# Output weights in two loads around the last values, all heads joined in one way, and two biases loaded late in 32 pieces

## The chip, the cores and the metric

The kernel runs on one core of a Trainium2 chip. The time is device microseconds of one execution. A core has TensorE (matrix products; it reads weights by a load of its own, PEld in the profile), VectorE (DVE), ScalarE (ACT), GpSimd (POOL) and SyncE (SP), which here only issues loads and waits. Loads from HBM run on the core's 16 DMA engines. Each engine works through its own instructions in order; between engines the program synchronises with semaphores.

## The reference

One decoding step of a transformer layer for two sequences (B = 2), in float32: attention of 32 heads over a cache of 8192 keys and values of width 128, then a feed-forward layer with the squared ReLU, each with a layer norm (without gain) before it and the input added behind it.

```
x1 = layernorm(x)                                  # (2, 512)
q = x1 @ wq                                        # 32 heads of 128
p = softmax(q . k_cache * 128 ** -0.5)             # over 8192 keys
h = x + concat_heads(p @ v_cache) @ wo             # wo: (4096, 512)
z = layernorm(h) @ w1 + b1                         # w1: (512, 1792)
out = h + (max(z, 0) ** 2) @ w2 + b2               # w2: (1792, 512)
```

A pair is one head of one sequence; there are 64 pairs, numbered 0 to 63, the two sequences of a head next to each other. Each pair has 4 MB of keys and 4 MB of values; all inputs are 561 MB.

## The kernel before

Everything streams through three buffers of 64 KB per partition, `ring[0]` to `ring[2]`. First `wq` is loaded into `ring[2]`, and the small inputs (x, b1, b2, 26 values per partition) into `sm` through ScalarE's queue; then one load of 8 MB per pair, keys and values together. A loop over SyncE waits for the semaphore FREE, which VectorE raises when it has finished with a buffer, and issues the load of the pair two ahead. Pair 63 comes in pieces: its keys alone (`kld`, into `ring[0]`, L239 multiplies them), then `wo` into `ring[1]`, then its values in five pieces (`vld`, semaphores LV), then, into `ring[2]`, W1 in two pieces (3 and 1 of its 4 row blocks of 128) and W2 in four (8, 4, 1 and 1 of 14 blocks). All of these are issued by SyncE in this order and go through one queue.

Per pair, with the keys in two chunks of 4096: TensorE forms the scores (L239), spread over the 128 partitions as four groups of 32 equal rows with 1024 keys each; VectorE takes each row's negated maximum (L245, into `nm`); ScalarE forms the exponentials with their sums (L249, `ls`); VectorE multiplies them with the values and sums along the row (L254), four products per chunk, one for each 32 of the 128 value columns, eight per pair, into `ac`.

So each pair has eight partial maxima and sums. They are joined behind the loop. `stats` takes the common maximum (TensorE with `pick` at L291, VectorE at L294 and L298, ScalarE's exponential at L301) and leaves weights `wt`; `sums` and `invert` form the total of a pair and its inverse `rl` (L306, L310, L315); `folded` weights and adds the value sums and brings them into columns (L321, L324, L327). This is done twice: first for the 62 pairs of heads 0 to 30, while the last pair's values are coming in, and then, between and behind the last pair's eight products, for the two pairs of head 31.

The result of the first 62 pairs is spread 16 times (`big`, L337) and multiplied with the 31 heads of `wo` (L344), which gives the attention output as rows, spread over four groups of 32 partitions. ScalarE copies it (L348), TensorE adds the groups and turns it to columns (L351), VectorE adds it to x, in `hT` (L366). This addition stands in VectorE's queue behind the third of the last pair's eight products. Head 31 is multiplied separately (L379, L382) and added (L385). `centre` subtracts the mean (L178 to L182), `spread` forms the variance (L187 to L195), whose inverse root `rstd` is applied only behind the product with W1 (L396), as is b1 (L407 to L414). W2's products (L421) add to `h + b2`, which is put in their accumulator ahead of them (L401, L405). A copy (L426) and a store (L428) end the kernel.

The order of work on each engine is the order in which the program is written; no scheduler changes it. `take` (L61) waits for a semaphore and lowers it again.

Of the kernel before, what the change touches and what calls it, by code (L numbers as in the profile page):

```python
# [11 lines left out]
P = 128  # L12
# [15 lines left out]
W1_PIECES = [3, 1]  # L28
V_PIECES = [(0, 2), (2, 4), (4, 6), (6, 7), (7, 8)]
# [34 lines left out]
def attention_block_kernel(nc, small, kvd, wqd, kld, vld, wod, w1d, w2d, out):  # L64
# [7 lines left out]
    NS = DB * B + FB + DB  # L72
    sm = sbuf("sm", NS)
    xT = sm[:, : DB * B].rearrange("p (a b) -> p a b", b=B)
    b1T = sm[:, DB * B : DB * B + FB]
    b2T = sm[:, DB * B + FB :]
# [20 lines left out]
    o31 = sbuf("o31", B)  # L97
    xr = sbuf("xr", DB, 16, B)
    hT = sbuf("hT", DB, B)
# [15 lines left out]
    SM, LK = p.sem("small"), p.sem("k63")  # L115
    LV = [p.sem(f"v63_{k}") for k in range(len(V_PIECES))]
# [5 lines left out]
    def load(tile, src, sem):  # L122
        sp.dma_start(tile, src).then_inc(sem, 16)

# [15 lines left out]
    load(ring[2], kvd[LAST - 1], LD[2])  # L140
    p.take(sp, FREE)
    load(ring[0][:, :HALF], kld, LK)
    p.take(sp, FREE)
    load(ring[1], wod, LD[1])
    for k, (a, b) in enumerate(V_PIECES):
        load(ring[0][:, HALF + a * CS : HALF + b * CS], vld[:, a * CS : b * CS], LV[k])
    p.take(sp, FREE)
    at = 0
    for k, n in enumerate(W1_PIECES):
        load(W1[:, at : at + n], w1d[:, at : at + n], LW1[k])  # L150
        at += n
    at = 0
# [20 lines left out]
    t_c = p.tell("dve", dve.tensor_reduce(fold, ident.rearrange("p (j m) -> p m j", j=NQ), axis=AX.X, op=ALU.add))  # L173
    dve.sem_inc(BUFFER, 3)

    def centre(src, tok, bank):
        p.after("dve", tok)
        tok = p.tell("dve", dve.tensor_reduce(part, src.rearrange("p d b -> p b d"), axis=AX.X, op=ALU.add))  # L178
        p.after("pe", tok)
        tok = p.tell("pe", pe.matmul(bank[:, :B], ones_d, part, start=True, stop=True))  # L180
        p.after("dve", tok)
        tok = p.tell("dve", dve.tensor_tensor(xc, src, bank[:, None, :B].to_broadcast([P, DB, B]), op=ALU.subtract))  # L182
        p.after("dve", tok)
        return tok

    def spread(bank):
        tok = p.tell("dve", dve.tensor_tensor(sq, xc, xc, op=ALU.mult))  # L187
        p.after("dve", tok)
        tok = p.tell("dve", dve.tensor_reduce(part, sq.rearrange("p d b -> p b d"), axis=AX.X, op=ALU.add))
        p.after("pe", tok)  # L190
        tok = p.tell("pe", pe.matmul(bank[:, :B], ones_d, part, start=True, stop=True))  # L191
# [3 lines left out]
        tok = p.tell("dve", dve.reciprocal(rstd, rstd))  # L195
        return tok
# [3 lines left out]
    tok = centre(xT, t_c, pm[0])  # L200
    tok = spread(pm[1])
# [83 lines left out]
    t_m = p.tell("dve", dve.tensor_copy(hT, xT))  # L285

    def stats(lo, nb):
        n2 = slice(lo * NC, (lo + nb) * NC)
        p.after("pe", t_m)
        for j in range(NQ):  # L290
            ins = pe.matmul(pm[0][:, j * nb * NC : (j + 1) * nb * NC], pick[:, j, :], nm[:, n2], start=True, stop=True)  # L291
        tok = p.tell("pe", ins)
        p.after("dve", tok)
        tok = p.tell("dve", dve.tensor_reduce(gm[:, lo : lo + nb], pm[0][:, : NQ * nb * NC].rearrange(  # L294
            "p (j i c) -> p i j c", j=NQ, c=NC), axis=AX.XY, op=ALU.min))
        p.after("dve", tok)
        w3 = wt[:, n2].rearrange("p (i c) -> p i c", c=NC)
        tok = p.tell("dve", dve.tensor_tensor(w3, gm[:, lo : lo + nb, None].to_broadcast([P, nb, NC]),  # L298
                                              nm[:, n2].rearrange("p (i c) -> p i c", c=NC), op=ALU.subtract))
        p.after("act", tok)  # L300
        return p.tell("act", act.activation(wt[:, n2], wt[:, n2], AF.Exp))  # L301

    def sums(lo, nb, tok):
        n2 = slice(lo * NC, (lo + nb) * NC)
        p.after("dve", tok)
        tok = p.tell("dve", dve.tensor_tensor(lw[:, n2], ls[:, n2], wt[:, n2], op=ALU.mult))  # L306
        p.after("pe", tok)
        l3 = lw[:, n2].rearrange("p (i c) -> p i c", c=NC)
        for c in range(NC):
            ins = pe.matmul(pm[1][:, :nb], pick_all, l3[:, :, c], start=(c == 0), stop=(c == NC - 1))  # L310
        return p.tell("pe", ins)

    def invert(lo, nb, tok):
        p.after("dve", tok)
        return p.tell("dve", dve.reciprocal(rl[:, lo : lo + nb], pm[1][:, :nb]))  # L315

    def folded(lo, nb):
        aw4 = aw[:, lo * NC * NH : (lo + nb) * NC * NH].rearrange("p (i c e) -> p i c e", c=NC, e=NH)
        ac4 = ac[:, lo * NC * NH : (lo + nb) * NC * NH].rearrange("p (i c e) -> p i c e", c=NC, e=NH)
        w4 = wt[:, lo * NC : (lo + nb) * NC].rearrange("p (i c) -> p i c", c=NC)[:, :, :, None].to_broadcast([P, nb, NC, NH])  # L320
        tok = p.tell("dve", dve.tensor_tensor(aw4, ac4, w4, op=ALU.mult))  # L321
        p.after("dve", tok)
        as3 = acs[:, lo * NH : (lo + nb) * NH].rearrange("p (i e) -> p i e", e=NH)
        tok = p.tell("dve", dve.tensor_tensor(as3, aw4[:, :, 0, :], aw4[:, :, 1, :], op=ALU.add))  # L324
        p.after("pe", tok)
        for e in range(NH):
            ins = pe.matmul(pm[0][32 * e : 32 * e + 32, :nb], fold, as3[:, :, e], start=True, stop=True)  # L327
        return p.tell("pe", ins)

    tok = stats(0, NG)  # L330
    tok = sums(0, NG, tok)
    tok = invert(0, NG, tok)
    p.after("dve", tok)
    tok = folded(0, NG)
    p.after("dve", tok)
    o4 = big[:, : HG * 32].rearrange("p (h r b) -> p h r b", r=16, b=B)
    tok = p.tell("dve", dve.tensor_tensor(  # L337
        o4, pm[0][:, :NG].rearrange("p (h b) -> p h b", b=B)[:, :, None, :].to_broadcast([P, HG, 16, B]),
        rl[:, :NG].rearrange("p (h b) -> p h b", b=B)[:, :, None, :].to_broadcast([P, HG, 16, B]), op=ALU.mult))
    p.after("pe", tok)  # L340
    p.take(pe, LD[1], 16)
    for h in range(HG):
        j = h % NQ
        ins = pe.matmul(pm[1][32 * j : 32 * j + 32, :], big[:, h * 32 : h * 32 + 32], WO[:, h, :],  # L344
                        start=(h < NQ), stop=(h + NQ >= HG))
    tok = p.tell("pe", ins)
    p.after("act", tok)
    tok = p.tell("act", act.activation(acc, pm[1], AF.Copy))  # L348
    p.after("pe", tok)
    for d in range(DB):  # L350
        ins = pe.matmul(pm[0][:, d * B : (d + 1) * B], acc[:, d * P : (d + 1) * P], fold[:, :B], start=True, stop=True)  # L351
    t_h = p.tell("pe", ins)


    order = [(c, e) for c in range(NC) for e in range(NH)]
    t_w = t_l = None
    piece = {a: k for k, (a, b) in enumerate(V_PIECES)}
    for n, (c, e) in enumerate(order):
# [15 lines left out]
    t_v = p.tell("dve", ins)  # L374
    t_z = p.tell("act", act.activation(s[2][:, :P], zero.to_broadcast([P, P]), AF.Copy))
    p.after("dve", t_v)
    tok = folded(NG, B)
    p.after("dve", tok)
    tok = p.tell("dve", dve.tensor_tensor(o31, pm[0][:, :B], rl[:, NG:BH], op=ALU.mult))  # L379
    p.after("pe", tok)  # L380
    for d in range(DB):
        ins = pe.matmul(pm[1][:, d * B : (d + 1) * B], WO[:, H - 1, d * P : (d + 1) * P], o31, start=True, stop=True)  # L382
    tok = p.tell("pe", ins)
    p.after("dve", tok)
    tok = p.tell("dve", dve.tensor_tensor(hT, hT, pm[1][:, : DB * B].rearrange("p (d b) -> p d b", b=B), op=ALU.add))  # L385
    tok = centre(hT, tok, pm[0])
    tok = p.tell("dve", dve.tensor_copy(xr, xc[:, :, None, :].to_broadcast([P, DB, 16, B])))
    p.after("pe", tok)
    y = s[0][:, :FQ]
    o = s[2][:, :P]  # L390
    at_d = 0
    for k, n in enumerate(W1_PIECES):
# [6 lines left out]
        if k == 0:  # L399
            t_r = spread(pm[1])  # L400
            t_b = p.tell("dve", dve.tensor_tensor(hb, hT, b2T[:, :, None].to_broadcast([P, DB, B]), op=ALU.add))  # L401
# [6 lines left out]
    p.after("dve", tok)  # L408
# [54 lines left out]
```

## Time and profile before

| What | Time |
|---|---|
| Median of three runs | 1309.69 us (1308.71 to 1312.11) |
| Profiled execution | 1312.31 us |
| its span, first to last instruction | 1309.7 us |
| TensorE busy | 410.1 us (31%) |
| VectorE busy | 759.0 us (58%) |
| ScalarE busy | 160.2 us (12%) |
| Mean DMA rate over the span | 428 GB/s |

The shares are means over the span; what an engine waits for has to be read stage by stage. In a row of a timeline the first two numbers are the start and the duration in us, then come engine, line, operation, what is written and read, and in brackets the idle time before it with what ended it. `DVEq`, `PEq` and `SPq` are the sequencers of the engines; a wait at L61 is mostly for a load. Rows for stretches of time give busy time of PE, PEld, DVE, ACT and POOL with numbers of instructions, then the granted TensorE clock as a share of the full one, the mean busy share of the 16 DMA engines, and GB/s. A product in float32 stands as two matmul records.

### The profile page before, as it was taken

The page shows a single profiled execution, that of the slowest core. Times are in us where ns is not written, and L with a number is a line of the kernel's source. Part 1 is how long each engine was busy: PE and PEld are TensorE (multiplying, and loading weights), DVE is VectorE, ACT ScalarE, POOL GpSimd, SP SyncE. Part 2 cuts the span into 40 slices and gives each one's busy share as a digit, 9 for nine tenths or more (in the row PEclk, how much of TensorE's full clock was granted, in tenths as well). Part 3 has the DMA queues.
Part 4 walks back from the last instruction along what each step waited for, and adds up shares of the span by engine and source line. Part 5 has one row for each costly group of instructions (what it writes and reads, how often), then busy time and mean ns, then how long its engine had stood idle before and what let it go on. Part 6 is the DMA issues. An engine that isn't in the chain of part 4 may idle for free. (4 is left out here: it accounts for less than half of the span.)

```text
span 1309.7 us, 8250 instructions
## 1 busy us (share of the span) xinstructions
PE 410.1 (31%) x2390; PEld 112.6 (9%) x2390; DVE 759.0 (58%) x1227; ACT 160.2 (12%) x267; POOL 0.7 (0%) x6
## 2 busy tenths in 40 slices
PE   2323223323323323332331332332232233133156
PEld 0100000000000000000000000000000000000013
DVE  1465575565566466557556556655645755664663
ACT  0011011011111111101101111110110110111110
POOL 0000000000000000000000000000000000000000
PEclk9766566656666566656666666766666675666667
DMA  9999999999999999999999999999999999999996
GB/s 417 417 447 422 442 438 426 444 422 444 420 444 420 446 418 446 420 444 436 428 444 420 446 420 444 420 444 420 446 418 446 428 436 442 422 444 422 430 423 271
DMA packets 11381, 561.14 MB, mean 428 GB/s; under 512 B 1392, under 2 KB 1520, under 8 KB 2160
## 3 DMA queue, kind: packets, MB, share of 16 engines
q1 hardware_dynamic: 11232, 561.06, 99.1%
q8 instruction: 3, 0.05, 0.0%
q10 hardware_dynamic: 144, 0.01, 0.0%
q14 instruction: 2, 0.02, 0.0%
HBM read 561.00 MB, written 0.07 MB: 428 GB/s over the span
## 5 line engine op out<-in xcount | busy, mean ns | idle before, releaser
L239 PE MATMUL s<-ring,qc 128*32 128x512 f32 x2048 | 369.8, 888 | 852.0 <-PEq L61 852.0
L254 DVE SCALAR_TENSOR_TENSOR ring<-ring,s 128x1024 f32<-128x1024 f32 x512 | 589.5, 1217 | 3.7 <-DVEq L61 3.6
L245 DVE TENSOR_REDUCE nm<-s 128x1024 f32 (+1 forms) x128 | 156.7, 1225 | 488.4 <-DVEq L61 488.4
L249 ACT ACTIVATE s<-s,nm 128x1024 f32<-128x1024 f32 x128 | 139.3, 1088 | 1081.8 <-ACTq L61 1081.8
L239 PEld LDWEIGHTS s<-ring,qc 128*32 128x32 f32 x2048 | 93.0, 155 | 1128.5 <-issue 1128.5
L254 DVE DVE_READ_ACCUMULATOR ring<-ring,s (+1 forms) x512 | 42.5, 83 | 0.0
L249 ACT ACTIVATION_READ_ACCUMULATOR s<-s,nm (+1 forms) x128 | 24.7, 193 | 0.0
L178 DVE TENSOR_REDUCE part<-sm 128x2 f32<-128x8 f32 x1 | 0.2, 161 | 19.3 <-DVEq L61 19.3
L344 PE MATMUL pm<-ring,big 128*32 128x512 f32 x62 | 10.0, 798 | 2.4 <-PEq L61 2.4
L216 PE MATMUL s<-ring,xr 128*32 128x512 f32 x64 | 9.7, 773 | 2.3 <-issue 2.3
L180 PE MATMUL pm<-part,ones_d 128*128 128x2 f32 x4 | 1.2, 363 | 23.6 <-DVE part L178 23.6
L221 DVE STREAM_TRANSPOSE big<-s 128x512 f32<-128x512 f32 x2 | 1.4, 718 | 9.1 <-PE s L216 9.1
L396 PE MATMUL s<-ring,xr 128*32 128x448 f32 x32 | 5.9, 886 | 0.6 <-issue 0.6
L270 DVE COPY qc<-qs 128x96 f32 x21 | 5.1, 243 | 0.0
L195 DVE RECIPROCAL rstd<-rstd 128x2 f32<-128x2 f32 x2 | 0.3, 166 | 7.7 <-ACT rstd L193 7.7
L291 PE MATMUL pm<-nm,pick 128*128 128x124 f32 (+1 forms) x16 | 3.3, 357 | 4.5 <-DVE hT L285 4.3
L193 ACT ACT_TABLE_LOAD x1 | 1.3, 1283 | 25.1 <-PE pm L191 25.1
L421 PE MATMUL s<-ring,a 128*2 128x128 f32 x112 | 3.2, 272 | 1.3 <-issue 1.3
L310 PE MATMUL pm<-lw,pick_all 128*128 128x62 f32 (+1 forms) x8 | 2.1, 395 | 4.6 <-DVE lw L306 4.6
L344 PEld LDWEIGHTS pm<-ring,big 128*32 128x32 f32 x62 | 2.6, 139 | 9.1 <-issue 9.1
L366 DVE TENSOR_TENSOR hT<-hT,pm 128x8 f32<-128x8 f32 x1 | 0.2, 164 | 5.6 <-PE pm L351 5.6
L291 PEld LDWEIGHTS pm<-nm,pick 128*128 128x128 f32 x16 | 2.9, 271 | 5.7 <-DVE hT L285 5.4
(63 smaller groups left out, 37.1 us busy)
## 6 DMA issues: line engine op xcount, KB each, us to landing
ring<-in_kld SPq DMA_DIRECT2D x1, 4096.0 KB, 31.1
ring<-in_vld SPq DMA_DIRECT2D x3, 1024.0 KB, 36.3
ring<-in_w1d SPq DMA_DIRECT2D x1, 2688.0 KB, 28.7
ring<-in_w2d SPq DMA_DIRECT2D x1, 2048.0 KB, 35.1
ring<-in_vld SPq DMA_DIRECT2D x2, 512.0 KB, 39.7
ring<-in_w2d SPq DMA_DIRECT2D x1, 1024.0 KB, 34.1
ring<-in_kvd SPq DMA_DIRECT2D x63, 40.9
ring<-in_w1d SPq DMA_DIRECT2D x1, 896.0 KB, 30.5
```

The costliest lines, as they stand in the source:

```text
L216: ins = pe.matmul(s[0][32 * j : 32 * j + 32, n * 512 : n * 512 + 512], xs[:, d, :], ring[2][:, c0 : c0 + 512], start=(d == 0), stop=(d == ...
L221: tok = p.tell("dve", dve.transpose(big[:, n * 512 : n * 512 + 512], s[0][:, n * 512 : n * 512 + 512]))
L239: ins = pe.matmul(s[k][32 * j : 32 * j + 32, n * 512 : (n + 1) * 512], qc[:, u, :], slot[:, c0 : c0 + 512], start=True, stop=True)
L245: dve.tensor_reduce(at(nm, pair, NC, c, 1), s[k], axis=AX.X, op=ALU.max, negate=True).then_inc(MAXED, 1)
L249: act.activation(s[k], s[k], AF.Exp, bias=at(nm, pair, NC, c, 1), scale=1.0, accum_out=at(ls, pair, NC, c, 1)).then_inc(EXPED, 1)
L254: return dve.scalar_tensor_tensor(v, v, 1.0, s[k], op0=ALU.mult, op1=ALU.mult, accum_out=at(ac, pair, NC * NH, c * NH + e, 1))
L270: dve.tensor_copy(qc, qs[:, bass.ds(i + 3, 3)][:, :, None].to_broadcast([P, 3, 32])).then_inc(QUERY, 1)
L291: ins = pe.matmul(pm[0][:, j * nb * NC : (j + 1) * nb * NC], pick[:, j, :], nm[:, n2], start=True, stop=True)
L310: ins = pe.matmul(pm[1][:, :nb], pick_all, l3[:, :, c], start=(c == 0), stop=(c == NC - 1))
L344: ins = pe.matmul(pm[1][32 * j : 32 * j + 32, :], big[:, h * 32 : h * 32 + 32], WO[:, h, :], start=(h < NQ), stop=(h + NQ >= HG))
L396: ins = pe.matmul(y[32 * j : 32 * j + 32, :], xs[:, d, :], W1[:, d, j * FQ : (j + 1) * FQ], start=(d == 0), stop=(d == DB - 1))
L421: ins = pe.matmul(o[32 * j : 32 * j + B, :], a2[:, m, :], W2[:, m, j * P : (j + 1) * P], start=False, stop=(m == FB - 1))
```

## The change

Loads. `sm` holds x alone. b2 is loaded by SyncE behind pair 62's keys and values, before it waits for the buffer of the last keys; b1 behind W1 and before W2. Each comes in 16 loads of 15, 14, 13 and so on to 1, and then 8 partitions, of 16 bytes (b2) or 56 bytes (b1) per partition, each with a semaphore of its own. `wo` comes as 24 heads ahead of the last values and 8 heads behind them; the last values come in three pieces (3, 3 and 2 products' worth) instead of five, W1 in 2 + 2 row blocks instead of 3 + 1.

Joining. The maxima, weights and totals of all 64 pairs are formed at once, behind the last pair's maxima; VectorE first waits for b2's 16 semaphores and adds b2 to x (`xb`). `folded` still runs twice, for 62 pairs and for the last two, but both end in `big`. The projection with `wo` runs for heads 0 to 23, then, behind the last pair's `folded`, for 24 to 30 and 31, all in the same accumulator. VectorE's last eight products follow each other with only the waits for values between.

Layer norm. ScalarE's copy of the projected rows also sums them; one more product of these sums with a constant matrix `foldm` gives the mean, so that `hc` (the centred x plus the attention output) minus the mean is written straight into `xr`. The variance comes from `xr`. `h + b2` is one addition of `xb`. Before the transposition behind W1, VectorE waits for b1's 16 semaphores. The load of ScalarE's square root table and the zeroing of W2's accumulator move ahead of the products.

The core of the diff:

```diff
-W1_PIECES = [3, 1]
-V_PIECES = [(0, 2), (2, 4), (4, 6), (6, 7), (7, 8)]
+W1_PIECES = [2, 2]
+V_PIECES = [(0, 3), (3, 6), (6, 8)]
+HA = 24
+ROW_PIECES = [15, 14, 13, 12, 11, 10, 9, 8, 7, 6, 5, 4, 3, 2, 1, 8]
...
+    def load_rows(tile, src, sems):
+        at = 0
+        for n, sem in zip(ROW_PIECES, sems):
+            load(tile[at : at + n], src[at : at + n], sem)
+            at += n
...
     load(ring[2], kvd[LAST - 1], LD[2])
+    load_rows(b2T, bias2, LB2)
     p.take(sp, FREE)
     load(ring[0][:, :HALF], kld, LK)
     p.take(sp, FREE)
-    load(ring[1], wod, LD[1])
+    load(WO[:, :HA], wod[:, :HA], LD[1])
     for k, (a, b) in enumerate(V_PIECES):
         load(ring[0][:, HALF + a * CS : HALF + b * CS], vld[:, a * CS : b * CS], LV[k])
+    load(WO[:, HA:], wod[:, HA:], LO)
     p.take(sp, FREE)
...
+    load_rows(b1T, bias1, LB1)
...
-    t_m = p.tell("dve", dve.tensor_copy(hT, xT))
+    for sem in LB2:
+        p.take(dve, sem, 16)
+    t_m = p.tell("dve", dve.tensor_tensor(xb, xT, b2T[:, :, None].to_broadcast([P, DB, B]), op=ALU.add))
...
+    def projected(lo, hi):
+        for h in range(lo, hi):
+            j = h % NQ
+            ins = pe.matmul(pm[1][32 * j : 32 * j + 32, :], big[:, h * 32 : h * 32 + 32], WO[:, h, :],
+                            start=(h < NQ), stop=(h + NQ >= H))
+        return ins
...
+    tok = folded(0, NG)
     p.after("pe", tok)
     p.take(pe, LD[1], 16)
+    projected(0, HA)
...
     for n, (c, e) in enumerate(order):
...
         ins = product(c, LAST, c, e, ring[0])
-        if n == 2:
-            p.after("dve", t_h)
-            t_h = p.tell("dve", dve.tensor_tensor(hT, hT, pm[0][:, : DB * B].rearrange("p (d b) -> p d b", b=B), op=ALU.add))
-            t_m = t_h
-            t_w = stats(NG, B)
-        if n == 4:
-            t_l = sums(NG, B, t_w)
-            act.activation(warm, eps_t, AF.Sqrt)
-        if n == 5:
-            t_l = invert(NG, B, t_l)
...
+    t_o = folded(NG, B)
+    p.take(pe, LO, 16)
+    projected(HA, HG)
+    p.after("pe", t_o)
+    tok = p.tell("pe", projected(HG, H))
+    p.after("act", tok)
+    tok = p.tell("act", act.activation(acc, pm[1], AF.Copy, accum_out=rows))
...
+    mean = s[2][:, 512 : 512 + B]
+    t_n = p.tell("pe", pe.matmul(mean, rows.to_broadcast([P, P]), foldm, start=True, stop=True))
+    tok = p.tell("dve", dve.tensor_tensor(hc, xc, h3, op=ALU.add))
+    tok = p.tell("dve", dve.tensor_tensor(xr, hc[:, :, None, :].to_broadcast([P, DB, 16, B]),
+                                          mean[:, None, None, :].to_broadcast([P, DB, 16, B]), op=ALU.subtract))
...
+    for sem in LB1:
+        p.take(dve, sem, 16)
     p.after("dve", t_y)
     tok = p.tell("dve", dve.transpose(yT, y))
```

More of the change, by code (lines that the diff above doesn't have):

```diff
@@ L61, in take, with attention_block_kernel @@
         engine.wait_ge(sem, n).then_inc(sem, -n)
-def attention_block_kernel(nc, small, kvd, wqd, kld, vld, wod, w1d, w2d, out):
+def attention_block_kernel(nc, small, bias1, bias2, kvd, wqd, kld, vld, wod, w1d, w2d, out):
     p = Program(nc)
@@ L71, in attention_block_kernel @@
     ring = [sbuf(f"ring{s}", ROW) for s in range(3)]
[L72 to L76, printed above, removed]
+    sm = sbuf("sm", DB * B)
+    xT = sm.rearrange("p (a b) -> p a b", b=B)
+    b1T = sbuf("b1T", FB)
+    b2T = sbuf("b2T", DB)
     ones_d = sbuf("ones_d", P)
@@ L96, in attention_block_kernel @@
     acc = sbuf("acc", D)
-    o31 = sbuf("o31", B)
+    rows = sbuf("rows", 1)
+    foldm = sbuf("foldm", B)
+    xb = sbuf("xb", DB, B)
+    hc = sbuf("hc", DB, B)
     xr = sbuf("xr", DB, 16, B)
-    hT = sbuf("hT", DB, B)
     hb = sbuf("hb", DB, B)
@@ L115, in attention_block_kernel @@
     SM, LK = p.sem("small"), p.sem("k63")
+    LO = p.sem("wo_b")
+    LB1 = [p.sem(f"bias1_{k}") for k in range(len(ROW_PIECES))]
+    LB2 = [p.sem(f"bias2_{k}") for k in range(len(ROW_PIECES))]
     LV = [p.sem(f"v63_{k}") for k in range(len(V_PIECES))]
@@ L173, in attention_block_kernel, with squares, root @@
     t_c = p.tell("dve", dve.tensor_reduce(fold, ident.rearrange("p (j m) -> p m j", j=NQ), axis=AX.X, op=ALU.add))
+    p.after("dve", t_c)
+    t_c = p.tell("dve", dve.tensor_scalar(foldm, fold[:, :B], 1.0 / D, None, op0=ALU.mult))
     dve.sem_inc(BUFFER, 3)
-    def centre(src, tok, bank):
+    def squares(src, tok):
         p.after("dve", tok)
-        tok = p.tell("dve", dve.tensor_reduce(part, src.rearrange("p d b -> p b d"), axis=AX.X, op=ALU.add))
-        p.after("pe", tok)
-        tok = p.tell("pe", pe.matmul(bank[:, :B], ones_d, part, start=True, stop=True))
+        tok = p.tell("dve", dve.tensor_tensor(sq, src, src, op=ALU.mult))
         p.after("dve", tok)
[L182 to L189, printed above, removed]
+        return p.tell("dve", dve.tensor_reduce(part, sq.rearrange("p d b -> p b d"), axis=AX.X, op=ALU.add))
+    def root(bank, tok):
         p.after("pe", tok)
@@ L194, in spread @@
         p.after("dve", tok)
-        tok = p.tell("dve", dve.reciprocal(rstd, rstd))
-        return tok
+        return p.tell("dve", dve.reciprocal(rstd, rstd))
     p.after("act", t_c)
     p.take(dve, SM, 16)
-    tok = centre(xT, t_c, pm[0])
-    tok = spread(pm[1])
+    p.after("dve", t_c)
+    tok = p.tell("dve", dve.tensor_reduce(part, xT.rearrange("p d b -> p b d"), axis=AX.X, op=ALU.add))
+    p.after("pe", tok)
+    tok = p.tell("pe", pe.matmul(pm[0][:, :B], ones_d, part, start=True, stop=True))
+    p.after("dve", tok)
+    t_x = p.tell("dve", dve.tensor_tensor(xc, xT, pm[0][:, None, :B].to_broadcast([P, DB, B]), op=ALU.subtract))
+    tok = root(pm[1], squares(xc, t_x))
     p.after("dve", tok)
@@ L284, in attention_block_kernel @@
         maxes(c, LAST, c)
-    t_m = p.tell("dve", dve.tensor_copy(hT, xT))
[L287 to L315, printed above, removed]
+    for sem in LB2:
+        p.take(dve, sem, 16)
@@ new lines, in attention_block_kernel, with by_pair @@
+    t_m = p.tell("dve", dve.tensor_tensor(xb, xT, b2T[:, :, None].to_broadcast([P, DB, B]), op=ALU.add))
+    def by_pair(t):
+        return t.rearrange("p (i c) -> p i c", c=NC)
+    p.after("pe", t_m)
+    for j in range(NQ):
+        ins = pe.matmul(pm[0][:, j * BH * NC : (j + 1) * BH * NC], pick[:, j, :], nm, start=True, stop=True)
+    tok = p.tell("pe", ins)
+    p.after("dve", tok)
+    tok = p.tell("dve", dve.tensor_reduce(gm, pm[0].rearrange("p (j i c) -> p i j c", j=NQ, c=NC), axis=AX.XY, op=ALU.min))
@@ new lines, in attention_block_kernel @@
+    p.after("dve", tok)
+    tok = p.tell("dve", dve.tensor_tensor(by_pair(wt), gm[:, :, None].to_broadcast([P, BH, NC]), by_pair(nm), op=ALU.subtract))
+    p.after("act", tok)
+    tok = p.tell("act", act.activation(wt, wt, AF.Exp))
+    act.activation(warm, eps_t, AF.Sqrt)
+    t_z = p.tell("act", act.activation(s[2][:, :P], zero.to_broadcast([P, P]), AF.Copy))
+    p.after("dve", tok)
+    tok = p.tell("dve", dve.tensor_tensor(lw, ls, wt, op=ALU.mult))
+    p.after("pe", tok)
+    for c in range(NC):
+        ins = pe.matmul(pm[1][:, :BH], pick_all, by_pair(lw)[:, :, c], start=(c == 0), stop=(c == NC - 1))
@@ L317, in folded @@
+    tok = p.tell("pe", ins)
+    p.after("dve", tok)
+    t_l = p.tell("dve", dve.reciprocal(rl, pm[1][:, :BH]))
     def folded(lo, nb):
@@ L319, in folded @@
         ac4 = ac[:, lo * NC * NH : (lo + nb) * NC * NH].rearrange("p (i c e) -> p i c e", c=NC, e=NH)
-        w4 = wt[:, lo * NC : (lo + nb) * NC].rearrange("p (i c) -> p i c", c=NC)[:, :, :, None].to_broadcast([P, nb, NC, NH])
+        w4 = by_pair(wt[:, lo * NC : (lo + nb) * NC])[:, :, :, None].to_broadcast([P, nb, NC, NH])
         tok = p.tell("dve", dve.tensor_tensor(aw4, ac4, w4, op=ALU.mult))
@@ L327, in folded @@
             ins = pe.matmul(pm[0][32 * e : 32 * e + 32, :nb], fold, as3[:, :, e], start=True, stop=True)
[L328 to L333, printed above, removed]
-    tok = folded(0, NG)
[L335 to L339, printed above, removed]
+        tok = p.tell("pe", ins)
+        p.after("dve", tok, t_l)
+        n = nb // B
+        return p.tell("dve", dve.tensor_tensor(
+            big[:, lo * 16 : (lo + nb) * 16].rearrange("p (h r b) -> p h r b", r=16, b=B),
+            pm[0][:, :nb].rearrange("p (h b) -> p h b", b=B)[:, :, None, :].to_broadcast([P, n, 16, B]),
+            rl[:, lo : lo + nb].rearrange("p (h b) -> p h b", b=B)[:, :, None, :].to_broadcast([P, n, 16, B]), op=ALU.mult))
+    def projected(lo, hi):
[4 more added lines that the diff above has]
+        return ins
+    tok = folded(0, NG)
     p.after("pe", tok)
     p.take(pe, LD[1], 16)
[L342 to L352, printed above, removed]
+    projected(0, HA)
     order = [(c, e) for c in range(NC) for e in range(NH)]
-    t_w = t_l = None
     piece = {a: k for k, (a, b) in enumerate(V_PIECES)}
@@ L363, in attention_block_kernel @@
         ins = product(c, LAST, c, e, ring[0])
-        if n == 2:
-            p.after("dve", t_h)
-            t_h = p.tell("dve", dve.tensor_tensor(hT, hT, pm[0][:, : DB * B].rearrange("p (d b) -> p d b", b=B), op=ALU.add))
-            t_m = t_h
-            t_w = stats(NG, B)
-        if n == 4:
-            t_l = sums(NG, B, t_w)
-            act.activation(warm, eps_t, AF.Sqrt)
-        if n == 5:
-            t_l = invert(NG, B, t_l)
[L374 to L377, printed above, removed]
-    p.after("dve", tok)
-    tok = p.tell("dve", dve.tensor_tensor(o31, pm[0][:, :B], rl[:, NG:BH], op=ALU.mult))
+    tok = p.tell("dve", ins)
+    p.after("dve", tok)
+    t_o = folded(NG, B)
[3 more added lines that the diff above has]
+    tok = p.tell("pe", projected(HG, H))
+    p.after("act", tok)
+    tok = p.tell("act", act.activation(acc, pm[1], AF.Copy, accum_out=rows))
     p.after("pe", tok)
+    h2 = pm[0][:, : DB * B]
     for d in range(DB):
[L382 to L387, printed above, removed]
+        ins = pe.matmul(h2[:, d * B : (d + 1) * B], acc[:, d * P : (d + 1) * P], fold[:, :B], start=True, stop=True)
+    t_h = p.tell("pe", ins)
+    mean = s[2][:, 512 : 512 + B]
+    t_n = p.tell("pe", pe.matmul(mean, rows.to_broadcast([P, P]), foldm, start=True, stop=True))
+    h3 = h2.rearrange("p (d b) -> p d b", b=B)
+    p.after("dve", t_h)
+    tok = p.tell("dve", dve.tensor_tensor(hc, xc, h3, op=ALU.add))
+    p.after("dve", t_n, tok)
+    tok = p.tell("dve", dve.tensor_tensor(xr, hc[:, :, None, :].to_broadcast([P, DB, 16, B]),
+                                          mean[:, None, None, :].to_broadcast([P, DB, 16, B]), op=ALU.subtract))
     p.after("pe", tok)
+    t_q = squares(xr[:, :, 0, :], tok)
+    t_b = p.tell("dve", dve.tensor_tensor(hb, xb, h3, op=ALU.add))
     y = s[0][:, :FQ]
@@ L399, in attention_block_kernel @@
         if k == 0:
-            t_r = spread(pm[1])
-            t_b = p.tell("dve", dve.tensor_tensor(hb, hT, b2T[:, :, None].to_broadcast([P, DB, B]), op=ALU.add))
+            t_r = root(pm[1], t_q)
     t_y = p.tell("pe", ins)
@@ L405, in attention_block_kernel @@
         pe.matmul(o[32 * j : 32 * j + B, :], hb[:, j, :], ident, start=True, stop=False)
+    for sem in LB1:
+        p.take(dve, sem, 16)
     p.after("dve", t_y)
     tok = p.tell("dve", dve.transpose(yT, y))
-    p.after("dve", tok)
+    p.after("dve", tok, t_r)
     y3 = yT.rearrange("p (m r) -> p m r", r=32)
@@ L445 @@
     arrays = {
-        "small": np.concatenate([x, a(B_b1).reshape(NQ, FB, 32).transpose(0, 2, 1).reshape(P, FB), a(B_b2).reshape(DB, P).T], axis=1),
+        "small": x,
+        "bias1": a(B_b1).reshape(NQ, FB, 32).transpose(0, 2, 1).reshape(P, FB),
+        "bias2": a(B_b2).reshape(DB, P).T,
         "kvd": np.concatenate([k[:LAST], v[:LAST]], axis=2),
@@ L450 @@
         "vld": v[LAST],
-        "wod": a(A_wo).reshape(H, DH, D).transpose(1, 0, 2).reshape(P, H * D),
+        "wod": a(A_wo).reshape(H, DH, D).transpose(1, 0, 2),
         "w1d": a(B_w1).reshape(DB, P, F).transpose(1, 0, 2),
```

## The prediction

> **What bounds the kernel now.** I read the page's totals first, then the stage table, then the chain that ended last, then the loads. No engine is near full, the transfers are:
>
> ```profile
> span 1309.7 us, 8250 instructions
> PE 410.1 (31%) x2390; PEld 112.6 (9%) x2390; DVE 759.0 (58%) x1227; ACT 160.2 (12%) x267; POOL 0.7 (0%) x6
> ```
>
> The stage table (engines' busy time, then TensorE clock, DMA share, GB/s) says where that stops being true:
>
> ```profile
> 60.00:1230.00 1170.00, 353.17 (x1952) 89.05 (x1952) 700.48 (x1102) 145.19 (x241) 0.00 (x0) 0.63 1.00 434
> ...
> 1260.00:1290.00 30.00, 16.88 (x102) 8.57 (x102) 14.53 (x30) 5.10 (x10) 0.00 (x0) 0.64 0.99 417
> ...
> 1297.00:1298.00 1.00, 1.00 (x8) 0.22 (x4) 0.00 (x0) 0.00 (x0) 0.00 (x0) 0.50 0.78 279
> ...
> 1298.80:1299.20 0.40, 0.40 (x8) 0.22 (x4) 0.00 (x0) 0.00 (x0) 0.00 (x0) 0.50 0.19 72
> ...
> 1299.60:1300.00 0.40, 0.40 (x8) 0.17 (x4) 0.00 (x0) 0.00 (x0) 0.00 (x0) 0.50 0.00 0
> ```
>
> All input is in by about 1299.9 us; until 1298 nearly all 16 DMA engines move, and in the last 1.6 us a fifth of them (three). The remaining 9.8 us are computation that came too late. The change leaves the 561 MB as they are, so the stream is a floor, and the gain can only be in those 9.8 us. The chain through them, from the landing of the output weights on (start, duration, what):
>
> ```profile
> 1272.52 10.02 PE pm L344 x62
> ...
> 1282.55 0.61 ACT acc L348
> ...
> 1283.20 1.07 PE pm L351 x8
> ...
> 1287.19 1.22 DVE ring L254 x3
> ...
> 1290.87 1.23 DVE ring L254 x3
> ...
> 1293.12 1.88 PE pm L382 x8
> ...
> 1295.43 0.59 PE pm L180 x2
> ...
> 1296.59 4.71 PE s L396 x24
> ...
> 1301.29 0.52 PE pm L191 x2
> 1301.81 1.16 PE s L396 x8
> ...
> 1304.46 3.28 PE s L421 x112
> ...
> 1307.77 0.29 DVE res L426
> ```
>
> After the projection of 31 heads (L344) VectorE still has five of the last pair's eight products (L254) to do: they stand in its queue behind the sum hT at L366, which waits for that projection. Everything behind them is late by that.
>
> **The loads.** SyncE's issues (start, duration), and KB and time to landing:
>
> ```profile
> 1202.14 0.34 SPq L123 DMA_DIRECT2D ring<-in_kvd  x1
> 1221.91 0.34 SPq L123 DMA_DIRECT2D ring<-in_kld  x1
> 1240.16 0.33 SPq L123 DMA_DIRECT2D ring<-in_wod  x1
> 1240.54 2.32 SPq L123 DMA_DIRECT2D ring<-in_vld  x5
> 1260.18 0.80 SPq L123 DMA_DIRECT2D ring<-in_w1d  x2
> 1261.02 14.11 SPq L123 DMA_DIRECT2D ring<-in_w2d  x4
> 1308.08 0.35 SPq L428 DMA_DIRECT2D out<-res  x1
> ...
> ring<-in_kld SPq DMA_DIRECT2D x1, 4096.0 KB, 31.1
> ...
> ring<-in_w1d SPq DMA_DIRECT2D x1, 2688.0 KB, 28.7
> ring<-in_w2d SPq DMA_DIRECT2D x1, 2048.0 KB, 35.1
> ...
> out<-res SPq DMA_DIRECT2D x1, 64.0 KB, 1.5
> ...
> ring<-in_wod SPq DMA_DIRECT2D x1, 32.2
> ```
>
> Last keys land at 1221.9 + 31.1 = 1253.0, output weights (8192 KB) at 1240.2 + 32.2 = 1272.4, so 8192 KB take 19.4 us, or 2.42 us per 1024 KB. W1's first 2688 KB land at 1260.2 + 28.7 = 1288.9, so the values ahead of them end 6.4 us earlier, at 1282.5, and W1's last 896 KB 2.1 us later, at 1291.0; W2's first 2048 KB at 1261.0 + 35.1 = 1296.1 and its last at about 1299.9.
>
> **The change, part by part.**
>
> *Output weights in 24 + 8 heads with the values between.* Same bytes, other order: 24 heads are 6144 KB, in at 1253.0 + 14.5 = 1267.5. The values come 3, 3 and 2 x 512 KB: 1271.2, 1274.8, 1277.2. The other eight heads follow at about 1282.5, where the values ended before.
>
> *One soft-max weighting for all 64 pairs.* 124 columns become 128. Before, it is this (start, duration):
>
> ```profile
> 1260.44 2.35 DVE L245 TENSOR_REDUCE nm<-s 128x1 f32<-128x1024 f32 x2 [0.40 <-DVEq L61]
> ...
> 1270.17 1.19 DVE L337 TENSOR_TENSOR big<-pm,rl 128x992 f32<-128x992 f32 x1 [0.56 <-PE pm L327]
> ...
> L61 DVEq EVENT_SEMAPHORE  x262: 21/21/21, 22.9 to 1289.8; - x131
> ```
>
> It ends at 1271.4, and with 3% more columns still by 1271.5. The copy of eight columns behind the maxima becomes a sum of eight columns behind 16 more waits. A wait is 21 ns by the last row; with dispatch I take 50 ns, 0.8 us, which passes while the second maximum (1.2 us of the 2.35) still runs. If that cover were missing, 0.8 us come on a step that has slack: the products behind it are weighted 0.5 us before they are needed (below). The second weighting of the last pair alone goes away, and with it the two halts inside the products.
>
> *The products.* VectorE starts them at 1271.5, 1.2 us each (1290.87 to 1292.1): 1281.0, as all three pieces are in time. The weighting of the pair then takes what it takes before between 1292.1 and 1293.12, 1.0 us: 1282.0. So the last values are no longer the limit; the second load of output weights at 1282.5 is.
>
> *Projection.* The 48 records of 24 heads run from 1271.5 and are done by 1280.5 even at the pace of before (62 in 10.02 us). What is left at 1282.5 is 8 heads, 16 records. Their price depends on the granted clock:
>
> ```profile
> 1272.50:1278.44 5.94, 5.92 (x28) 1.56 (x32) 3.33 (x5) 0.00 (x0) 0.00 (x0) 0.50 1.01 416
> 1278.44:1282.60 4.16, 4.06 (x38) 1.07 (x30) 0.26 (x2) 0.05 (x1) 0.00 (x0) 1.00 1.04 429
> ...
> 1296.50:1301.20 4.70, 4.61 (x24) 1.12 (x24) 0.22 (x2) 0.00 (x0) 0.00 (x0) 0.50 0.33 122
> ...
> 1304.40:1307.80 3.40, 3.24 (x112) 2.90 (x112) 0.04 (x1) 0.00 (x0) 0.00 (x0) 1.00 0.00 0
> ```
>
> Half clock 0.21 us a record, full clock 0.11. TensorE will have idled about 2 us, as it had before 1285, so I take half: 3.4 us, to 1286.0. Evacuation 0.61 plus the read-out of the row sums now collected with it, 0.2:
>
> ```profile
> L249 ACT ACTIVATION_READ_ACCUMULATOR s<-s,nm (+1 forms) x128 | 24.7, 193 | 0.0
> ```
>
> That is 1286.9. Back to columns, 8 small products: 1.07 us at full clock, 1.88 for eight such (L382) at half; I take 1.9: 1288.8. The mean is one more product, 0.6 like L180; the sum hc goes beside it. Then xr, an estimated 0.3 us from L180's neighbours at 1296.02 to 1296.59: 1289.7. L382 and the separate mean of hT (L178 to L182) go.
>
> *W1 in 2 + 2.* Its first half (1792 KB) lands at 1286.8, before 1289.7: no wait. 16 records at half clock (24 in 4.71) 3.1: 1292.8. The variance product 0.5, second half (in since 1291.0) 3.1: 1296.4. From there the chain of before holds, 1302.97 to 1304.46, 1.5 us: W2's products start at 1297.9. W2's first part is in, the last comes at 1299.9. 3.28 us: 1301.2. As before, 2.0 us follow (1304.46 + 3.28 to 1309.7). End 1303.1, which is 6.6 us less. With the full clock everywhere, the last piece of W2 would be the limit: 1299.9 + 0.3 + 2.0 = 1302.2, 7.5 us less. If W2's 112 records too ran at half clock, 3.3 us more: 1306.4, 3.3 less.
>
> *The biases, 32 small loads.* Issue: 0.33 to 0.46 us each by the rows above (five in 2.32), so 5 to 7.5 us for 16. The first group is issued after 1202.5 and SyncE has nothing to do until 1221.9; the second before W2's, whose data is needed from 1291 on. The issue itself is hidden up to 1.2 us per load. What the pieces cost in the stream no row shows. One engine may get a row and a completion from each of 16 pieces, for each bias: 32 times both. Lower bound, from the old load of small inputs:
>
> ```profile
> q10 hardware_dynamic: 144, 0.01, 0.0%
> ```
>
> under 0.05% of 16 x 1309.7 us is under 10.5 us for 144 packets, under 73 ns each; pipelined row and completion cost 0 to 0.15 us together, 0 to 4.7 us on that engine. Upper bound: if each piece waits for its own landing, the lone output store's 1.5 - 0.35 = 1.15 us, 37 us. I take the lower row, since these are reads under running traffic as that one was, and in its range a low value, 0.05 us, as 73 ns is what the rounding leaves and no measurement: 1.6 us, about what most engines have spare against the slowest three (1298 to 1299.6 above). Net: 0. A gain below zero is possible only as far as those three lose their share of the old small load, under 0.3 us.
>
> The Trainium skill (DMA: Bandwidth & Descriptors, section Rules for kernel authors) speaks against it: many small transfers should be coalesced into one large one. Its section Anatomy of one DMA gives about 2.0 us of fixed cost per DMA, fitted for loads issued by GpSimd, where these come from SyncE; 32 of them in series would be an estimated 64 us. This trace has 12 loads landing between 1260 and 1300 with the DMA share at 0.99 to 1290, so such a cost overlaps here, at least for loads of 256 KB and more; for loads of a few rows no run here shows it.
>
> **Against the median.** The profiled execution took 1312.31 us (span 1309.7 and 2.6 around it), 0.2% over the median 1309.69. I take the 6.6 us off the median: 1303.1.
>
> **Rivals.**
> 1. *The small loads go one landing at a time* on one DMA engine, and every later load waits for that engine. With price c per piece, the end moves by 32c - 1.6. The gain is eaten at c = 0.25; slower by 0.3% (3.9 us) from c = 0.38 us; at 1.15 it would be 1338. For it: nothing here shows small loads back to back. Against it: W2's last three loads, 1536 KB, end 3.8 us after its first, and the rate alone makes it 3.6. The Trainium skill (same title, section Queues, rings and completion order) says the semaphore write lands only after every earlier write of that engine, which is how this could come about; no run here shows a stall by it.
> 2. *SyncE's queue fills.* W2's four issues took 14.11 us with eight loads outstanding. If it is the number of loads that blocks, the first 16 pieces hold up the keys' issue till 1241.6 and then the last eight pieces' issue, 8 x 0.4 = 3 us of stream, is lost, and as much again ahead of W2: 6 us, time 1309. Against it: those four issues were over by 1275.1, when only the weights (1272.4) and at most one piece of the values (2.4 us later) had landed, so it is not one landing per issue.
> 3. *TensorE stays at half clock throughout:* 3.3 us gained, 1306.4.
>
> **How the numbers follow.** What a measurement of this kernel can tell is about 0.3%, 3.9 us: faster is under 1305.8, slower over 1313.6. Forecast (1301.5 to 1305.5) 0.58; rival 3 in between, half of it still faster, 0.14; rival 2 and rival 1 with c near 0.25 (1306 to 1313) 0.13; rival 1 beyond 0.38, 0.15. Faster 0.58 + 0.07 + 0.03 = 0.68, same 0.17, slower 0.15. The range goes from just under the full-clock floor (1302.2, and 0.7 for the spread of the runs) to 1310, with 0.18 left out above. The forecast's own range is that of its case.
>
> **What would show it.** DMA share falling to zero at 1299 to 1301, and under 4 us after it to the end (9.8 now); all eight last products in one run, starting near 1271.5; the last eight heads starting at the second load's landing near 1282.5; W2's products starting before 1298.5; the waits for biases under 0.3 us. Wrong if the keys land later than 1254, or a hole in the DMA share stands near 1242 or 1291, or W2 lands after 1302.

## The result and the profile after

Over 20 runs of each, the changed kernel takes 1307.93 us and the kernel before 1310.47 us, medians; the ratio is 0.9981 (95% interval 0.9975 to 0.9988). It is faster, by 2.5 us and not by 6.6. The profiled execution took 1307.91 us with a span of 1306.2.

The computation went as forecast, and further. The rows of the changed kernel's timeline (start, duration, engine, line, what):

```profile
1263.15 0.16 DVE L302 TENSOR_TENSOR xb<-sm,b2T 128x8 f32<-128x8 f32 x1
...
1281.73 0.17 DVE L332 TENSOR_TENSOR aw<-ac,wt 128x16 f32<-128x16 f32 x1
...
1283.24 3.47 PE L350 MATMUL pm<-ring,big 128*32 128x512 f32 x16 [0.84 <-PEq L63]
1286.77 0.60 ACT L374 ACTIVATE acc<-pm 128x512 f32<-128x512 f32 x1 [18.26 <-PE pm L350]
...
1287.51 1.05 PE L378 MATMUL pm<-fold,acc 128*128 128x2 f32 x8 [0.81 <-ACT acc L374]
...
1289.27 2.73 PE L398 MATMUL s<-ring,xr 128*32 128x448 f32 x16 [0.48 <-issue]
...
1292.44 2.07 PE L398 MATMUL s<-ring,xr 128*32 128x448 f32 x16
...
1295.77 0.19 DVE L417 SCALAR_TENSOR_TENSOR a<-a 128x28 f32<-128x28 f32 x1
```

All is ready for W2 at 1295.96 us, where before it was 1304.4. But TensorE then stands still. The whole chain that ended last is these lines:

```profile
1299.33 0.04 issue
1299.37 4.95 PE s L424 x112
1304.32 0.02 issue
1304.34 0.29 DVE res L429
```

The chain begins at 1299.3, with the landing of W2's first part. SyncE's issues and the times to landing of the changed kernel:

```profile
1202.94 5.70 SPq L129 DMA_DIRECT2D b2T<-in_bias  x16
1220.66 0.36 SPq L129 DMA_DIRECT2D ring<-in_kld  x1
...
1261.46 10.61 SPq L129 DMA_DIRECT2D b1T<-in_bias  x16
1272.11 11.61 SPq L129 DMA_DIRECT2D ring<-in_w2d  x4
```

```profile
ring<-in_kld SPq DMA_DIRECT2D x1, 4096.0 KB, 33.2
...
ring<-in_w2d SPq DMA_DIRECT2D x1, 2048.0 KB, 27.1
```

```profile
L129 SPq DMA_DIRECT2D ring<-in_w2d x4: 351/3486/4161, 1272.1 to 1280.0; - x4
DMA to landing us min/median/max: 22.9/26.8/29.2
```

The keys land at 1220.66 + 33.2 = 1253.8 instead of 1253.0, W2's first part at 1272.1 + 27.1 = 1299.2 instead of 1296.1, its last at 1280.0 + 22.9 = 1302.9 instead of 1299.9. The bytes are the same, so something holds the stream up by 3 us. Stretches of time (the last three columns are TensorE clock, DMA share, GB/s) show how:

```profile
1297.00:1298.00 1.00, 0.00 (x0) 0.00 (x0) 0.00 (x0) 0.00 (x0) 0.00 (x0) 1.00 0.77 311
1298.80:1299.20 0.40, 0.00 (x0) 0.00 (x0) 0.00 (x0) 0.00 (x0) 0.00 (x0) 1.00 0.47 189
1299.60:1300.00 0.40, 0.40 (x24) 0.39 (x16) 0.00 (x0) 0.00 (x0) 0.00 (x0) 1.00 0.51 205
1302.00:1302.40 0.40, 0.40 (x16) 0.31 (x12) 0.00 (x0) 0.00 (x0) 0.00 (x0) 0.50 0.07 26
```

Before, the share fell from 0.78 (1297 to 1298) to 0.19 (from 1298.8) and to zero at 1299.6: thirteen engines ended nearly together. Now half of the engines still work at 1299.6 and one at 1302.2. The engines end one after another, and a load is complete when the last of them is: W2's first part lands on the first engine at 1294.0 and on the last at 1299.2, and TensorE starts at 1299.4. Landings on single engines, here and below, are the times at which each engine signals a load's semaphore in the trace.

### The profile page after: what moved, and what is told of

Its sections match the earlier page's. It is cut to its first block, busy times and chain, and to the rows that moved or that the text cites. A ratio compares the mean times of both kernels' runs of the same rounds, so it can differ in the third digit from the quotient of the medians.

```text
span 1306.2 us, 8270 instructions
## 1 busy us (share of the span) xinstructions
PE 411.9 (32%) x2372; PEld 110.4 (8%) x2372; DVE 757.6 (58%) x1221; ACT 160.2 (12%) x267; POOL 0.7 (0%) x6
## 5 line engine op out<-in xcount | busy, mean ns | idle before, releaser
L253 PE MATMUL s<-ring,qc 128*32 128x512 f32 x2048 | 375.7, 900 | 848.7 <-PEq L63 848.7
L424 PEld LDWEIGHTS s<-ring,a 128*2 128x2 f32 x112 | 3.9, 109 | 5.7 <-issue 4.9
## 6 DMA issues: line engine op xcount, KB each, us to landing
ring<-in_kld SPq DMA_DIRECT2D x1, 4096.0 KB, 33.2
ring<-in_w2d SPq DMA_DIRECT2D x1, 2048.0 KB, 27.1
```

The lines of the kernel that those rows point to most:

```text
L253: ins = pe.matmul(s[k][32 * j : 32 * j + 32, n * 512 : (n + 1) * 512], qc[:, u, :], slot[:, c0 : c0 + 512], start=True, stop=True)
L424: ins = pe.matmul(o[32 * j : 32 * j + B, :], a2[:, m, :], W2[:, m, j * P : (j + 1) * P], start=False, stop=(m == FB - 1))
```

## The experiments

Three theories. Theory 1 is the prediction's first rival in a mild form: the small loads pass one after another on a DMA engine, at some 0.18 us each. That is the spacing at which one engine completes its pieces of b1 in the trace of the changed kernel (the last engine twelve of them from 1291.92 to 1293.94). Theory 2: the 16 issues ahead of W2 make SyncE late (W2's issues begin at 1272.1 instead of 1261.0). Theory 3: the new order and cutting of the large loads costs stream time. Ratios are to the kernel before, on the same chip.

**Biases early, the rest of the change kept.**

```diff
+    sm = sbuf("sm", DB * B + FB + DB)      # x, b1 and b2 in one load at the start, as before
-    load_rows(b2T, bias2, LB2)
-    load_rows(b1T, bias1, LB1)
-    for sem in LB2: p.take(dve, sem, 16)   # and the same for LB1
```

> The changed kernel with both biases back in the one small load at the start; everything else of the change stays. Theory 1 (the 16 small pieces pass one after another on a DMA engine, 0.18 us each, and delay all later loads on it): W2's last landing back from 1302.9 to about 1299.9 us, span about 1303, ratio to before 0.995. Theory 2 (SyncE issues W2 too late, 1272 to 1284 instead of 1261 to 1275): the same, since the 16 issues are gone. Theory 3 (the new order and cutting of the large loads costs stream time): W2's landing stays at 1302 to 1303, span about 1306, ratio 0.998.

Measured: 1303.6 us, ratio 0.9951 (0.9938 to 0.9965), span 1302.1. Its interval lies wholly below that of the changed kernel: the rest of the change gains 6.4 us, and the late biases cost 3.9 (0.0030 in the ratio; 4.1 between the spans). W2 in this kernel:

```profile
L128 SPq DMA_DIRECT2D ring<-in_w2d x4: 432/1807/4378, 1261.2 to 1266.6; - x4
DMA to landing us min/median/max: 33.0/35.6/36.7
```

```profile
1298.42 0.04 issue
1298.46 1.68 PE s L411 x48
1300.14 0.02 issue
1300.16 0.29 DVE res L416
```

The last piece lands at 1266.6 + 33.0 = 1299.6, as before the change, and the last product ends 0.6 us later. Theory 3 falls. This version beats both kernels.

**Each bias in one load, at the late places.**

```diff
-ROW_PIECES = [15, 14, 13, 12, 11, 10, 9, 8, 7, 6, 5, 4, 3, 2, 1, 8]
+ROW_PIECES = [128]
```

> The changed kernel with each bias in one load of 128 rows, at the places where the 16 loads stood. Theory 1, if the price hangs on the number of loads (completions) per engine: one completion in the place of 16, at most 0.4 us left, span about 1303.3. Theory 1, if the price hangs on the rows: 8 rows per engine and bias, 8 x 0.18 = 1.4 us twice, on all engines alike, span about 1305.5. Theory 2: two issues in the place of 32, span about 1303.

Measured: 1303.65 us, ratio 0.9953 (0.9940 to 0.9967), span 1302.2. Late places cost nothing, and 128 rows in one load cost nothing that can be seen: on the first engine to finish, b1 lands 0.21 us behind W1's second half, and W2's first part is 0.09 us later behind W1 than with the biases early. So the price hangs on the number of loads, not on the rows.

**One bias late at a time.** The other bias goes back to the small load at the start.

```diff
-    load_rows(b2T, bias2, LB2)      # first run: b1 alone stays late
-    load_rows(b1T, bias1, LB1)      # second run: b2 alone stays late
```

> The changed kernel with b2 back in the small load at the start and b1 still in 16 late pieces ahead of W2. Theory 1: half of the loss stays, W2's last landing about 1301.3, span about 1304.7, ratio 0.9965. Theory 2: the issues ahead of W2 are all there, so the whole loss stays: landing 1302.9, span 1306, ratio 0.998.

> The changed kernel with b1 back in the small load at the start and b2 still in 16 late pieces ahead of the last keys. Theory 1: half of the loss stays, keys about 1 us later than 1253.0, W2's last landing about 1301, span about 1304.5, ratio 0.9963. Theory 2: W2 is issued early as before, nothing is lost: landing 1299.9, span about 1303, ratio 0.995.

Measured: 1305.08 us, ratio 0.9965 (0.9951 to 0.9978) with b1 alone late, and 1305.93 us, 0.9965 (0.9952 to 0.9979) with b2 alone. W2's last piece lands at 1301.65 and 1301.31, against 1299.56 with both early and 1302.94 with both late. Each group costs about half, 1.8 us by the ratios; the intervals overlap that of the first experiment, but the landings lie apart. In the second run W2's issues begin at 1260.35, and it loses as much as the first: theory 2 is not what happens here. In the changed kernel too, the last of W2's issues is over at 1283.7, before the first engine has W1's first half (1284.8).

A second cause shows in the landings of single engines. Behind W1's first half, where no small load stands between two others, each engine keeps its distance to the first one within 0.1 us. But in both runs the slowest one falls back once: from 2.59 to 3.56 us between W1 and W2's first part with b2 alone late, from 3.08 to 4.01 between W2's first and second part with b1 alone late. Just then, from 1293.07 and from 1297.14, the trace has a packet of 8 KB on the queue q14, which brings instructions of the program. The pages count these packets over the span, of the changed kernel and of the one with the biases early:

```profile
q14 instruction: 2, 0.02, 0.0%
```

```profile
q14 instruction: 1, 0.01, 0.0%
```

The runs without a late packet (biases early, each bias in one load, and the last experiment) have no such step. The kernel before has one, at 1294.03, but there an engine with room fell back, from 0.91 to 1.89, and the last landing hardly moved. In the changed kernel the packet comes at 1293.61, and the slowest engine is then 1.0 us behind the next. So of the 3.4 us by which W2's last landing moved, an estimated 1.0 goes with this packet and 2.4 with the small loads themselves. That the packet takes the time is inferred from when it comes; no run moved it alone.

**The kernel before with late biases alone.**

```diff
     load(ring[2], kvd[LAST - 1], LD[2])
+    load_rows(b2T, bias2, LB2)             # b1 behind W1 likewise, the waits as in the changed kernel
```

> The kernel before with the bias part of the change alone: b2 and b1 each late in 16 pieces, nothing else. Theory 1: keys and output weights land about 1 us later, the chain behind the output weights starts that much later, W2 (3 us later) is still in time there: span about 1310.8, ratio 1.0008. Theory 2: W2 is issued later but needed only at 1304, nothing ahead of it moves: ratio 1.000.

Measured: 1313.38 us, ratio 1.0023 (1.0014 to 1.0032), span 1312.0. Worse than either theory expected, and for another reason. The output weights come 0.9 us later, as theory 1 had it, but the projection behind them ran 0.8 us faster at a better clock, and the product with W1 ends at 1302.6, no later than before (1303.0). The loss comes behind it, from a cost that I had put at nothing (start, duration):

```profile
1302.15 0.15 DVE L413 TENSOR_TENSOR hb<-hT,b2T 128x8 f32<-128x8 f32 x1
1303.87 0.65 DVE L421 STREAM_TRANSPOSE yT<-s 128x448 f32<-128x448 f32 x1 [1.57 <-DVEq L62]
```

Between these two VectorE works off the 16 waits for b1, all of which had landed by 1294.3, eight microseconds earlier; they follow each other 0.111 us apart, 1.8 us in all. 1.2 us of this lie on the path. Then W2's 112 records take 4.80 us instead of 3.28: the granted clock fell to 0.5 at 1305.02, while TensorE stood still: 2.4 us here, where the kernel before has 1.3 us and keeps the full clock. That the longer pause brought the clock down was not tested.

**Eight loads of 16 rows each.**

```diff
+ROW_PIECES = [16] * 8
```

> The changed kernel with each bias in 8 loads of 16 rows. If 16 rows go to 16 engines, every engine gets 8 rows and 8 completions per bias. Theory 1: 8 x 0.18 = 1.5 us per bias on all engines alike, the spread of a load's landings back to 1.7 us, W2's last landing about 1302.5, span about 1306. Theory 2: half the issues, W2 issued some 5 us earlier than in the changed kernel; half the loss at most, span about 1304.5.

Measured: 1304.99 us, ratio 0.9961 (0.9947 to 0.9974), span 1303.7. There are as many completions in all as in the changed kernel (128 per bias, and each load of n rows has n landings in both traces), but evenly spread, eight for each engine; there, one engine can have 16. The loss over the early biases is 1.3 us by the ratios against 3.9, and W2's last piece lands at 1273.1 + 28.0 = 1301.1, 1.6 us later than with the biases early. About 0.8 of these go with the instruction packet, which comes at 1297.53, when the lag of the slowest engine grows from 1.41 to 2.20; 0.8 are left for the small loads, against 2.4. So the number on the worst engine counts. How fast they pass:

```profile
L129 SPq DMA_DIRECT2D b1T<-in_bias x8: 419/420/432, 1261.7 to 1264.9; - x8
DMA to landing us min/median/max: 27.6/28.6/29.7
```

They land from 1261.7 + 29.7 = 1291.4 to 1264.9 + 27.6 = 1292.5, so 0.16 us apart; on the first engine to finish they are 0.18 us apart. What follows is held up by less: on that engine the keys come 0.88 us and W2's first part 0.68 us later behind their predecessors than with the biases early, 0.11 and 0.09 us per load. Theory 1 was right in the mechanism and had taken the spacing of the completions for the delay, nearly twice its size in this run.

**32 loads of 4 rows each.**

```diff
+ROW_PIECES = [4] * 32
```

> The changed kernel with each bias in 32 loads of 4 rows: the suspected cost doubled on four engines, with as many rows in all. Theory 1: 32 x 0.18 = 5.9 us per bias on four engines, against 2.9; W2's last landing about 1308 to 1309, span about 1312, ratio 1.002 to 1.003. If the cost hung on the total of rows, it would stay at 1306. Theory 2: twice the issues, W2 issued up to 10 us later, a hole in the DMA share of all engines ahead of W2's first packets.

Measured: 1314.63 us, ratio 1.0032 (1.0020 to 1.0044), span 1313.4. Slower than the kernel before. The size is about what theory 1 expected. Of the 16 engines four end W1's second half 5.2 to 7.6 us after the first one; with the biases early the slowest is 2.1 us behind. The keys' last landing moves from 1252.78 to 1257.48, 4.7 us for 32 loads or 0.15 us each on the engines that have them. SyncE now is late as well:

```profile
1261.34 29.75 SPq L129 DMA_DIRECT2D b1T<-in_bias  x32
1291.13 3.16 SPq L129 DMA_DIRECT2D ring<-in_w2d  x4
```

```profile
1290.00:1292.00 2.00, 1.50 (x8) 0.00 (x0) 0.00 (x0) 0.44 (x1) 0.00 (x0) 0.50 0.25 108
```

Its issues take 0.93 us each where 16 took 0.66, W2 is issued only at 1291.1, and the DMA share is 0.25 from 1290 to 1292: the hole that theory 2, and the prediction's second rival, spoke of. With 16 loads it is not there (1.13 in the changed kernel over the same two microseconds). The landings show which of the two sets the end. On the slowest engine b1's pieces land from 1296.5 to 1302.2, after W2 was issued, so W2 stands behind the pieces there and not behind SyncE. The twelve engines for which there was a hole (0.25 is four engines of 16) have all of W2 by 1302.9, seven microseconds before the last part of it lands at 1310.0. So the hole is real, but it costs nothing here. In the same way the 32 issues of b2 hold up the keys' issue from 1220.5 to 1230.0, and the first engine has the keys at 1250.9 as with the biases early.

**Output weights in one load, biases early.**

```diff
+HA = 32
-    load(WO[:, HA:], wod[:, HA:], LO)
-    p.take(pe, LO, 16)
```

> As the first experiment (biases early), but the output weights in one load ahead of the last values, as before. What the two loads are worth: the weights land at 1272.4, the values at 1282.5, so the last two products and the weighting of the last pair end near 1286 and only one head is left to multiply, against eight heads from 1282.5 to 1286. If W2's landing at 1299.9 sets the end either way, no difference: span about 1303. If the compute chain sets it, up to 1 us either way.

Measured: 1306.36 us, ratio 0.9965 (0.9952 to 0.9979), span 1304.9: slower than with two loads by 1.8 us in the ratio, whose intervals just overlap, and by 2.8 between the spans; more than expected. The computation sets the end again, and at half clock:

```profile
1286.70 1.93 PE pm L337 x2
...
1289.39 1.87 PE pm L363 x8
...
1292.12 3.21 PE s L383 x16
...
1299.72 3.28 PE s L407 x112
```

W2's products start at 1299.7, when nearly all of W2 has landed (the last at 1299.4). With two loads they started at 1296.0. So taking the two loads away costs about 2 to 3 of the 6.4 us that the change without late biases gains; the rest belongs to the common joining and the shorter chain. Part of the 2 to 3 is the clock, which was at half until 1297.32 here and full from 1292.78 with two loads; that part was not separated.

## Why the prediction was wrong

*The step that failed* is the sum of the small loads: "in its range a low value, 0.05 us ... Net: 0". The range itself, 0 to 0.15 us per piece, was about right: a piece delayed what follows by 0.09 to 0.11 us where every engine has eight of a group, and by 0.15 on engines that have 32. What failed is the low value in it and the 1.6 us of room set against it. The late biases cost 3.9 us net, and the time fell among the cases from 1306 to 1313, which had been given 0.13. I had taken the nearest row to be the old small load with its 144 packets. It is one load with eight rows and one completion per engine; the second experiment shows that such a load passes in 0.2 us altogether. What the change adds is sixteen loads, and for a chain of loads on one engine there was no row. And the engine that ends last had no room: the pieces of b1 from 15 rows to four land last at an even 0.18 us, so it seems to be one engine, with twelve pieces at least.

Of the 4.1 us between the spans, W2's last landing makes 3.4 (1299.56 to 1302.94): an estimated 2.4 by the small loads and 1.0 with the packet of instructions, which the prediction did not have at all. The other 0.8 us are TensorE's: it idled from 1294.7 till 1299.4, fell to half clock at 1300.06, and ended 1.4 us behind the last landing instead of 0.6. The first rival had the mechanism. That its formula, 32c - 1.6, gives 4.2 us with c = 0.18 is luck: 0.18 us is the spacing of the completions and not the delay, and the formula has neither the packet nor TensorE's part.

The Trainium skill (DMA: Bandwidth & Descriptors, section Why a DMA increments its semaphore by 16 and not by 1) says that a load issued as these are runs on the k lowest-numbered engines and that only these report when their data has landed. The trace agrees on the number: beside one signal some 0.5 us after the issue, the pieces of 15, 14, 13 rows and so on have 15, 14, 13 landings. It does not name the engines. The Trainium skill's advice to coalesce (same title, section Rules for kernel authors) was right here. Its about 2.0 us per DMA (section Anatomy of one DMA), fitted for another way of issuing, would have been more than ten times too much: the pieces land 0.18 us apart.

*Point by point.* The stream as a floor, and 9.8 us behind it as the only place for a gain: right; with the biases early the span shrank by 7.6 us to 1302.1, against 1303.1 forecast and 1302.2 with full clock. Eight products in one run: from 1272.20 instead of 1271.5, since the first piece landed only at 1272.06, with one wait of 0.2 us for the second piece. Last eight heads at the second load's landing: 1283.24 for 1282.5, later because that load comes later with the biases; 1282.45 in the first experiment. Sixteen records at half clock: 3.47 for 3.4; TensorE had idled 2.9 and 0.8 us just before. The trace of the kernel before was misread on this point: ahead of its half clock at 1285.27 TensorE idled about 0.9 us and not 2. The return to columns took 1.05 and not 1.9 us, since the clock was full from 1286.41, and the clock was full again from 1293.23, in W1's second half: W2 could start at 1296.0 instead of 1297.9. A second mistake hardly showed: I had the waits at 50 ns each, and they are 111. In the changed kernel those for b1 run beside the second half of W1's product and end at 1294.6, 0.1 us after it, so they were still covered; in the fifth experiment 1.2 us of them were not. The first group was covered, as forecast: the sum xb starts at 1263.15, while the second maximum ran until 1263.24.

The keys landing under 1254 and no hole at 1242 or 1291 held. Of the signs for the forecast, the DMA share at zero by 1301 and W2's products before 1298.5 did not come; of the signs against it, the last one came: W2 landed after 1302.

## What to carry to other kernels

Count loads per DMA engine, not bytes: where a stream is the floor, one load of 128 rows cost 0.2 us on an engine, and two such loads in 16 pieces each made the last load land 3.4 us later, an estimated 2.4 of it by the pieces, because a load is complete only when its slowest engine is. A gain in a tail is worth what the loads that end it allow, so check a change that adds loads for the landing of the last one first, and look which engine of the 16 makes it late. A price taken from a row must come from a row of the same kind: one small load says little of sixteen in a chain.

## What the runs showed of the hardware that was not expected

Loads of a few rows back to back on one engine complete 0.16 to 0.18 us apart, and delay what follows by about 0.1 us each when all engines have eight of them, by 0.15 where a few engines have 32. A packet of 8 KB of the program's instructions coincides with one engine falling 0.8 to 1.0 us behind; it costs that where it falls on the engine that ends last. A wait on VectorE that is already satisfied costs 0.111 us of its sequencer when waits follow each other, though the profile gives the wait itself 21 ns. SyncE's issue of a small load took 0.36 us with little outstanding (16 in 5.70 us), 0.66 in the second group, and 0.93 when 32 were issued.
